# Attention and SwiGLU on one core: all transposes on TensorE instead of partly by DMA, and readouts split in two

## The chip, the cores and the metric

The kernel runs on one core of one Trainium2 chip. The metric is the device time of one execution in microseconds (us); a kernel's time is the median of its runs.

## The reference

Attention over 4 batches, 8 heads, 768 positions and a head dimension of 64, with two kinds of heads, and then a feed-forward block on the result. Everything is float32 in the reference; the kernel computes in float16 with float32 sums.

```python
scores = (q @ k^T) / sqrt(64)                       # q, k, v: (4, 8, 768, 64)
causal = row >= col
stream = causal & ((col < 4) | (row - col < 64))    # 4 sink keys, a window of 64
mask   = causal for heads 0, 2, 6; stream for the other five heads
a      = softmax(where(mask, scores, -1e9))
x      = (a @ v) as (3072 tokens, 512)
out    = (silu(x @ w_gate) * (x @ w_val)) @ w_out   # w_gate, w_val: 512 x 1536; w_out: 1536 x 512
```

## The kernel before

The 3072 tokens are 24 tiles `t` of 128 rows; two tiles make a pair `n` (12 pairs, in the order of `QP`), four tiles a group `g` (6 groups).

**Per pair.** `load` (L341) brings q, k and v of 256 rows into buffers of the ring `raw` (11 buffers, L169). `cast` (L429) writes q and k as float16 into a buffer `hq`. Then q and k have to be turned, so that the head dimension lies on the partitions. For pairs below `XPE = 5` (L336) that is done by TensorE: `transposes` (L469) issues 8 transposes of 128x128 for q and 8 for k into one PSUM bank each, and `evac` (L475) copies each bank out in two halves (ScalarE or VectorE). For pairs 5 to 11 it is done by DMA: `dmat` (L462) issues a transposing DMA on SyncE's queue, two for q and two for k of a pair. In the pairs whose turning is by DMA, q and k are loaded with 512 bytes in a run, one DMA each; pairs 1 to 4 are loaded with 2 KB in a run, two DMAs each, and cast into another order of columns (`XOLD <= n < XPE`).

**Per tile.** `scores` (L551) multiplies on TensorE into two PSUM banks (`sc`), `exps` (L569) takes the exponential on ScalarE into `e`, `mask` (L581) multiplies with 0 and 1 on VectorE or GpSimd, `values` (L591) multiplies with v, and `norm` (L600) divides by the sums and writes `xb`. Then `xb` is turned into `xt`, with the model dimension on the partitions: for tiles below `XBAR = 8` (L423) by `xtranspose` (L609) with 4 transposes on TensorE and one copy out of PSUM (`xevac`, L624), for tiles 8 to 23 by one transposing DMA (L615).

**Per group.** For each of 12 blocks `j` of the hidden dimension: `gate` (L755) with the gate weights, `tanh` (L763), `stt1` (L767), `gate` with the value weights, `stt2` (L773), which writes `h_sb`. The output product of groups 0 to 4 is done with seven block products instead of eight (`seventh`, L830, matmuls at L839), with sums of blocks of h made by `hsum` (L818, L826). The seven products are added up into `out_sb` by `gathered` (L850): `r1` is a plain copy; `c11`, `r6`, `r67`, `c21`, `r56`, `c22` and `c12` are VectorE additions of a PSUM bank and a cell of `out_sb` (L855). Group 5 has a plain product (`outproj`, L788). `store_half` and `store` write the result.

**The order of the work.** Nothing is scheduled while the kernel runs. Every piece above is a task of a plan; the string `ORDER` gives the order in which the tasks are issued, `WAYS` the engine of each, `SLOTS` its buffers. An engine works through its own instructions in that order, each waiting on semaphores. Tasks in `ORDER` that are no tasks of the plan are matmuls that only keep TensorE running (`warm`, L315). The 8 PSUM banks are shared by scores, values, gates, products and transposes.

Of the kernel before, what the change touches and what calls it, by code (L numbers as in the profile page):

```python
# [16 lines left out]
    "0306071W091U1V1X000A08xy1c0D0C01050B1d1e040gy01f1gzJ1i1h2021282922232B1j1r1s021p1q1w0F2C2D2E2F1b"  # L17
    "2A2L2M2N2O2X2f2g0m1Y1a1Z1t1u1v1k0h252h1l1m2W2c242G2H2I2d2e2l2m2i2j0G271n1o1y1z3C262P2Q2R0z2t3031"
    "2J0y8e8o2n2K102U2o2p3I3J2V8t8j8m8u8v8k8l8n1x2k8f8g8p8q2x382y8h8i118r8s8w8x138y8z9893909495999A33"
    "340n9D9E0E2Z3K3D3L3M3N149B9C9F969G9H972a9192322b2Y2q2r2s2u3R3S3W3X0k1C9c9d9e9h9i9j3U3V3O2z353P36"  # L20
    "39370q1D9f9g9k9l3T3b3i3n3o3f3g0H3H3E3F2v2w0i169I9J9K9N9O9P0o179L9Q9R9M0l1F3Q3Y3Z3c3j3a0I3u40410j"
    "193k3h9m9n9o3l3m3A3B9S9T9U9r9s9t3d3e9X0J3v4344453G3p3q3r0r1G9u9p9v429Y9Z3s3t0x1H2S4647494A4H0p1A"
    "9V9WB74N4O4Q4R0K3z9q9zA10N4c3x4BB4B5B6B8Ak4K4L4V4b4C4D3yAT484M0w0sAQARASAU9a9b9y0t1E0W6K2TAlAmAV"
    "AWAX151M1O1N1PAYAZBEAfAgAhB9BABB4a0u181Q1R1SBCBDAp0v1BBFBGA0AaAbAnAoAc3wBHBIAdAe0L0M0PB20T12A41I"
    "1J1K0S4d4P0O4Z4h4g4Y4e4f5D5L5K0RAzB0B1AqArB31L0YALAM0ZAN4E4F4G4J4I6J1TAuAvAOAPAw9wA2A69xA3A7A55C"
    "5I5JAA4l4m4i4j4kACA8A9ABAD4n4v51524y53AiAj5f5lAEBMAGAFAK4S4z504T4W4UAxAy5g5nAsAtBL4q4r4o4p54BO0c"
    "AHAIAJ4s554t4u4x4wBJBKBQ56575T5U6MBNBP5W5c5XBb5j0X58595A5B707S7T6xBVBW6wBRBS5i5VBXBYBc6z5YBZBaBd"
    "5p5qBT5s605t5u4XBsBtBuCeCbCcCdCfCMCNCOCCBvBwCDCE0V6I5v0Q5F5G5H6v5k5o5M5N5O0UBiBjBk5rCPCQBlBm5E5Z"
    "5a5b5d5wCHCICJCWCXCY5m63696A666768Bh5h73CKCLC7C8C9710eCRCS5P5Q5R6465CACBCTBUC2C36y7Q6P74BnBo5x5y"
    "5z610a72CZCaBp5S625e6H6NBqBrC46B6C6F6D6GCFCGCiBeBfBgBxByBz7O7UC0C1C5C681CUCVCjCl6E6U6V6W6X6Y6R6S"  # L30
    "6T6eDmDjDkDlDnDoDpDqDrDs0b7P7X7WDtDuDv6Z6aCgChCn6b6c6d6fDUDVDWDXDY7576776g7C7D7E7F7G7L0dDwDxCkCm"
    "DSDFDGDHDPDQDRDT7b7c7d6QDADBDCDyDzE0DDDE7H80D5D6D7CsCt6O6n6o6h6i6j6kE1E27V7I7J7M7K7ND8D96l6m7879"
    "7A7BCoCpCrCuCv897Y7Z6p6q8786DKDLDMDZDaDb6L6r6s6t6uDcDdDeDfDgCwCx7e7f7R7j7m7n7o7p7q7rDNDOCyCzD0D4"
    "EhEiEjErEsEcEd88EkElEtCqD1D2D3EuEvEeDhDi7a7g7h7k7iFLFMFNFOFP7x8D8E8A8I8B8C8F8JFJFGFHFIFKFBFCFDDI"
    "DJE5E77s7t8GFEFFEp7u7v7y7w8HEXEYEZ0f838485EmEnEoEqEfEg8NEw8Y8ZE6E88T8U8VEzExEyF0EBE3E9E4EAECEDF6"
    "828K8L8M8OF1F2F3F9EFEG8Q8R8S8W8XEVEHEIEJF7F8FA7l8P7z8a8b8cEaEbESETEUEWEEEOELEM8dGiGMGTGUEKGCENER"
    "G7GVGWGjGkGJGKEPGREQFTFVGXGLGOGPGEGFGNGQG9F4GAGSGGGYGbGZF5GaGcGBGDFSGHFpFqFrFQFRG4G5GdGeFzFUFeFW"
    "FXGIG6G0G8FcFdGfFfFuFvFYFaFbGgGhG1G2G3FsFtFxGlGmFZFwFyFlFiFjFmFnFgFhFkFoGnGoGpGsGtGuGvGwGqGrGxGy"
    "GzH0H2H3H4H5H7H1H6H8H9"
)  # L40
WAYS = (
    "000010000000000000000000000000000000000000000000000000000000221202202202212200200111000111110010"
    "222200001100000000000000220022122022001011000000000000001100212002000011001001000001000001001000"
# [76 lines left out]
def kernel(  # L120
# [45 lines left out]
    PAIRS = [(2, 6), (0, 4), (1, 5), (3, 7)]  # L166
    assert all(y == x + 4 for x, y in PAIRS)

    RINGS = {"raw": 11, "hq": 5, "e": 6, "xb": 3, "xt": 2, "sig": 2, "sil": 3,  # L169
             "ps": 8, "gv": 8, "o": 8, "big": 8}  # L170
    P = Plan(RINGS)

# [160 lines left out]

    XPE = 5  # L336
    XOLD = 1

    landed = {}
# [83 lines left out]
    XBAR = 8  # L423
# [596 lines left out]
```

## Time and profile before

| | |
|---|---|
| median of 3 runs | 246.04 us (245.84 to 246.38) |
| the profiled execution's own time | 246.15 us |
| its span, first to last instruction | 244.4 us |
| granted TensorE clock | 1.000 |
| TensorE busy | 234.5 us, 96% |
| VectorE busy | 186.7 us, 76% |
| ScalarE busy | 148.5 us, 61% |
| GpSimd busy | 129.0 us, 53% |
| DMA moved | 40.73 MB, 167 GB/s over the span |

In the profile PE is TensorE's matmul side, PEld its weight loads, DVE VectorE, ACT ScalarE, POOL GpSimd and SP SyncE, which here only issues DMAs. Matmuls overlap in a pipeline, so the busy time of PE is no measure of how full it is: the mean duration of a 512-column matmul is given as 379 ns, while one starts every 216 ns in a dense stretch. The chain of waits is followed back from the last instruction: each step to what released it, or to the instruction before it on its engine. "Issue" in it is time in which the profile shows nothing waited for.

### The profile page before, as it was taken

Reading aid. Unit: us, or ns where it says so; the run is one execution under the profiler, and the core shown is the slowest. Engines: PE = TensorE matmul, PEld = TensorE weight load, DVE = VectorE, ACT = ScalarE, POOL = GpSimd, SP = SyncE. Lnnn points to the kernel's source line nnn. Section 1 sums busy time; section 2 is a strip of 40 time slices with the busy share of each in tenths; the row PEclk is TensorE's granted clock in tenths of the full one; section 3 lists DMA queues with packets and bytes.
Section 4 is the critical chain, followed back from the end, with each engine's and each line's share of the span. In section 5 each row is a group of like instructions: output and inputs, shape, how many; then the busy total and the mean of one; then the engine's idle time right before and its main releaser. Section 6 shows DMA issues by size and latency. Waiting matters only on the chain.

```text
span 244.4 us, 5604 instructions
## 1 busy us (share of the span) xinstructions
PE 234.5 (96%) x2189; PEld 143.6 (59%) x2189; DVE 186.7 (76%) x324; ACT 148.5 (61%) x235; POOL 129.0 (53%) x140
## 2 busy tenths in 40 slices
PE   7989999998999999799999999999999999999995
PEld 3667855553457678445555457656456764475743
DVE  0577887889999999887987977669769777776800
ACT  3899899887878669487637776563682302330011
POOL 7479999956497552375765446910094110375000
PEclk9999999999999999999999999999999999999999
DMA  6999999999766989999464451519100213100053
GB/s 187 355 348 353 323 352 366 313 362 305 206 131 78 287 165 289 191 268 192 89 130 130 97 120 38 90 36 234 38 4 0 46 21 115 59 0 1 7 203 136
DMA packets 66794, 40.73 MB, mean 167 GB/s; under 512 B 25168, under 2 KB 60240, under 8 KB 66768
## 3 DMA queue, kind: packets, MB, share of 16 engines
q1 hardware_dynamic: 65392, 37.76, 61.5%
q10 hardware_dynamic: 1376, 2.62, 2.9%
q8 instruction: 17, 0.28, 0.5%
q14 instruction: 9, 0.07, 0.1%
HBM read 28.31 MB, written 6.29 MB: 142 GB/s over the span
## 4 chain that ended last, share of the span: by engine, by line
PE 54%; DVE 19%; issue 8%; DMA 6%; POOL 5%; SPq 5%; ACT 2%; DVEq 0%; POOLq 0%
PE banks L759 34%; PE banks L839 10%; PE banks L793 4%; DMA raw<-in_moe_w_val_dram 4%; DVE h_sb L775 4%; PE banks L567 3%; DVE h_sb L826 3%; SPq L349 3%; DVE sil L769 3%; PE banks L597 2%; POOL hs_sb L826 2%; DVE out_sb L855 2%; DVE xb L605 2%; DMA xt<-xb 2%; DVE e L587 2%
## 5 line engine op out<-in xcount | busy, mean ns | idle before, releaser
L759 PE MATMUL banks<-xt,wg_sb 128*128 128x512 f16 (+1 forms) x304 | 70.3, 368 | 1.9 <-DMA xt<-xb 1.4
L759 PE MATMUL banks<-xt,wv_sb 128*128 128x512 f16 (+1 forms) x304 | 70.4, 368 | 0.8 <-DVE sil L769 0.7
L579 ACT ACTIVATE e<-banks 128x1024 f16<-128x1024 f32 (+2 forms) x68 | 58.7, 910 | 20.0 <-PE banks L567 11.7
L765 ACT ACTIVATE sig<-banks 128x512 f32<-128x512 f32 (+1 forms) x76 | 43.0, 577 | 43.5 <-PE banks L759 37.5
L769 DVE SCALAR_TENSOR_TENSOR sil<-sig,banks 128x512 f32<-128x512 f32 (+1 forms) x76 | 49.0, 656 | 14.8 <-ACT sig L765 12.6
L775 DVE SCALAR_TENSOR_TENSOR h_sb<-sil,banks 128x512 f16<-128x512 f32 (+1 forms) x76 | 48.7, 656 | 6.7 <-PE banks L759 4.4
L587 POOL TENSOR_TENSOR e<-e,m 128x640 f16<-128x640 f16 (+1 forms) x22 | 37.8, 1727 | 27.2 <-ACT e L579 24.3
L759 PEld LDWEIGHTS <-wg_sb 128*128 128x128 f16 x304 | 28.5, 98 | 30.7 <-issue 3.1
L759 PEld LDWEIGHTS <-wv_sb 128*128 128x128 f16 x304 | 28.2, 98 | 29.5 <-issue 1.2
L839 PEld LDWEIGHTS <-h_sb 128*128 128x128 f16 x360 | 34.8, 98 | 7.9 <-issue 0.7
L826 POOL TENSOR_TENSOR hs_sb<-h_sb 128x768 f16<-128x768 f16 x7 | 11.5, 1640 | 40.9 <-DVE h_sb L775 29.4
L855 DVE TENSOR_TENSOR out_sb<-banks,out_sb 128x512 f32<-128x512 f32 x35 | 23.6, 685 | 4.7 <-PE banks L839 4.4
L826 POOL TENSOR_TENSOR h_sb<-h_sb 128x768 f16<-128x768 f16 x11 | 18.0, 1639 | 8.2 <-PE banks L839 4.4
L839 PE MATMUL banks<-wo_sb,h_sb 128*128 128x256 f16 x180 | 21.9, 273 | 0.0
L839 PE MATMUL banks<-wt_sb,h_sb 128*128 128x256 f16 x180 | 21.5, 273 | 0.4 <-DVE out_sb L855 0.4
L567 PE MATMUL banks<-qT,kT 64*128 64x128 f16 x472 | 20.6, 218 | 1.1 <-DVE xb L605 1.0
L567 PEld LDWEIGHTS <-kT 64*128 64x128 f16 x472 | 14.6, 94 | 11.0 <-issue 10.2
L597 PEld LDWEIGHTS <-e 128*128 128x128 f16 x472 | 17.1, 97 | 4.3 <-ACT vt L206 0.9
L597 PE MATMUL banks<-vt,e 128*128 128x65 f16 x472 | 18.2, 193 | 1.0 <-POOL vt L208 0.7
L605 DVE TENSOR_TENSOR xb<-banks,rc 128x512 f16<-128x512 f32 x24 | 16.6, 691 | 0.8
L208 POOL CAST vt<-raw 64x512 f16<-64x512 f32 x22 | 14.4, 654 | 4.8 <-DMA raw<-in_v_dram 2.3
L206 ACT COPY out_sb<-banks 128x512 f32<-128x512 f32 (+1 forms) x7 | 4.0, 570 | 19.1 <-PE banks L793 16.0
(60 smaller groups left out, 216.3 us busy)
## 6 DMA issues: line engine op xcount, KB each, us to landing
raw<-in_v_dram SPq DMA_DIRECT2D x12, 512.0 KB, 7.0
raw<-in_q_dram SPq DMA_DIRECT2D x8, 512.0 KB, 4.8
raw<-in_k_dram SPq DMA_DIRECT2D x8, 512.0 KB, 5.1
raw<-in_moe_w_gate_dram SPq DMA_DIRECT2D x6, 512.0 KB, 8.9
raw<-in_moe_w_val_dram SPq DMA_DIRECT2D x6, 512.0 KB, 8.4
raw<-in_moe_w_out_dram SPq DMA_DIRECT2D x6, 512.0 KB, 7.9
out_dram<-out_sb SPq DMA_DIRECT2D x6, 512.0 KB, 4.7
raw<-in_q_dram SPq DMA_DIRECT2D x8, 256.0 KB, 6.4
```

The lines of the kernel that those rows point to most:

```text
L567: nc.tensor.matmul(sc[:, c:c + n, :], weights, moving, start=first, stop=last)
L579: nc.scalar.activation(out=to, in_=src, func=AF.Exp, scale=scale)
L587: ENG[task().way].tensor_tensor(out=ev, in0=ev, in1=mm, op=ALU.mult)
L597: nc.tensor.matmul(avs[t][:, odd, n * 66:n * 66 + 65], ee, vv, start=(m == 0), stop=(m == len(bl) - 1))
L605: nc.vector.tensor_tensor(out=xb.rearrange("p n o d -> p o n d"), in0=av[:, :, :, 0:64], in1=rc.to_broadcast([128, 2, 4, 64]), op=ALU.mult)
L759: nc.tensor.matmul(ps, wsb[:, kk, j * 128:(j + 1) * 128], xt[:, kk, c[0]:c[1]], start=(kk == 0), stop=(kk == 3))
L765: nc.scalar.activation(out=sg[g, j, c], in_=gs[g, j, c], func=AF.Tanh, scale=0.5)
L769: nc.vector.scalar_tensor_tensor(out=sl[g, j, c], in0=sg.pop((g, j, c)), scalar=1.0, op0=ALU.add, in1=gs.pop((g, j, c)), op1=ALU.mult)
L775: nc.vector.scalar_tensor_tensor(out=hs[g, j][:, c[0]:c[1]], in0=sl.pop((g, j, c)), scalar=0.5, op0=ALU.mult, in1=vs.pop((g, j, c)), op1=A ...
L826: ENG[T_hs[g, x][part].way].tensor_tensor(out=to, in0=a, in1=b, op=op)
L839: nc.tensor.matmul(rooms[g, p][:, x], left[:, j, 128 * x:128 * x + 128], right[:, j], start=(j == 0), stop=(j == NK - 1))
L855: nc.vector.tensor_tensor(out=cell(*to), in0=rooms[g, p], in1=cell(*other), op=ALU.add)
```

## The change

- `XPE` becomes 12 and `XBAR` goes: q and k of all pairs and x of all tiles are turned by TensorE and copied out of PSUM. `dmat` and the transposing DMA of `xtranspose` go. With `XPE = 12`, q and k of pairs 5 to 11 are loaded in two DMAs with 2 KB runs, and the exponentials of their tiles write their columns in plain order.
- The additions `c11`, `c21` and `c12` of groups 0 to 4 become two tasks each: `fetched` copies the PSUM bank into a float32 buffer of a new ring `tmp` (two buffers) by ScalarE or VectorE, and `summed` adds that buffer and the cell of `out_sb` by GpSimd or VectorE. The PSUM bank is free after the copy.
- The ring `raw` has 10 buffers instead of 11.
- `ORDER`, `WAYS` and `SLOTS` are new as a whole.

What the new `WAYS` assign (number of tasks; before -> after):

| tasks | ScalarE | VectorE | GpSimd | SyncE |
|---|---|---|---|---|
| transposing DMAs of q and k | | | | 28 -> 0 |
| transposing DMAs of x | | | | 16 -> 0 |
| copies of turned k out of PSUM | 4 -> 15 | 6 -> 9 | | |
| copies of turned q out of PSUM | 8 -> 16 | 2 -> 8 | | |
| copies of turned x out of PSUM | 2 -> 8 | 6 -> 16 | | |
| `c11`, `c21`, `c12` as one addition | | 15 -> 0 | | |
| their copies (`fetched`) | 0 -> 6 | 0 -> 9 | | |
| their additions (`summed`) | | 0 -> 8 | 0 -> 7 | |

On TensorE, the tasks of 8 transposes go from 10 to 24, those of 4 transposes from 8 to 24, the `warm` matmuls inside the order from 11 to 14. Everything else on TensorE is the same in number and size. In the new order the first gate products again come after the scores and values of tiles 0 to 3, and the first load of value weights is again the eleventh load.

```diff
-    RINGS = {"raw": 11, "hq": 5, "e": 6, "xb": 3, "xt": 2, "sig": 2, "sil": 3,
+    RINGS = {"raw": 10, "hq": 5, "e": 6, "xb": 3, "xt": 2, "sig": 2, "sil": 3, "tmp": 2,
...
-    XPE = 5
+    XPE = 12
...
-    XBAR = 8
-
...
-    def dmat(n, kd, m):
-        nc.sync.dma_start_transpose(
-            out=turned(n, kd)[:, m].rearrange("c k r (j n) -> c (k r j) n", j=2),
-            in_=hqs[n, kd][m * 64:(m + 1) * 64].rearrange("p k a x -> p (k a x)"))
...
-        if t // 2 >= XPE:
-            to = to.rearrange("p c (n j) -> p c n j", j=2)
-            src = src.rearrange("p c (j n) -> p c n j", j=2)
         nc.scalar.activation(out=to, in_=src, func=AF.Exp, scale=scale)
...
-        if t >= XBAR:
-            nc.sync.dma_start_transpose(
-                out=xts[g][:, :, n * 128:(n + 1) * 128],
-                in_=xb.rearrange("p a b d -> p (a b d)"))
-            return
         tr = buf("gv", [128, 4, 128], FH, "xtr")
...
-            if n >= XPE:
-                T_ev[n, kd] = [P.lands(P.add(
-                    f"d{kd}{n}.{m}", ["SP"], (lambda n=n, kd=kd, m=m: dmat(n, kd, m)),
-                    deps=cs[kd] + old)) for m in range(2)]
-                P.uses(cs[kd][0], "hq", *T_ev[n, kd])
-                continue
...
+    APART, SINCE = ('c11', 'c21', 'c12'), 0
+
+    def fetched(g, name):
+        temps[g, name] = buf("tmp", [128, 2, HM], FP, "tmp")
+        copy(T_fe[g, name], temps[g, name], rooms[g, CELLS[name][0]])
+
+    def summed(g, name):
+        p, to, other = CELLS[name]
+        ENG[T_ga[g, name].way].tensor_tensor(out=cell(*to), in0=temps.pop((g, name)),
+                                             in1=cell(*other), op=ALU.add)
...
+            if name in APART and g >= SINCE:
+                T_fe[g, name] = P.add(f"fe{g}.{name}", ["ACT", "DVE"],
+                                      (lambda: fetched(g, name)), deps=deps[:1], takes=["tmp"])
+                T_ga[g, name] = P.add(f"oe{g}.{name}", ["POOL", "DVE"],
+                                      (lambda: summed(g, name)), deps=[T_fe[g, name]] + deps[1:])
+                P.uses(T_fe[g, name], "tmp", T_ga[g, name])
+                return T_ga[g, name]
...
-        P.uses(p2, "o", c11)
+        P.uses(p2, "o", T_fe.get((g, "c11"), c11))
...
-        P.uses(p4, "o", c21)
+        P.uses(p4, "o", T_fe.get((g, "c21"), c21))
...
-        P.uses(p3, "o", c12)
+        P.uses(p3, "o", T_fe.get((g, "c12"), c12))
```

## The prediction

> **What bounds the kernel now.** I read the page first, then stretches of the span, the chain of waits in order of time, and the groups.
>
> The page's first part:
>
> ```profile
> PE 234.5 (96%) x2189; PEld 143.6 (59%) x2189; DVE 186.7 (76%) x324; ACT 148.5 (61%) x235; POOL 129.0 (53%) x140
> ```
>
> Two stretches (columns: stretch, its length, then busy us and instruction count of PE, PEld, DVE, ACT, POOL, then clock, DMA share, GB/s):
>
> ```profile
> 60.00:100.00 40.00, 39.16 (x406) 27.35 (x404) 38.92 (x66) 29.84 (x44) 21.32 (x19) 1.00 0.90 188
> ...
> 200.00:241.40 41.40, 41.38 (x247) 23.40 (x244) 24.76 (x38) 9.29 (x16) 11.40 (x7) 1.00 0.19 71
> ```
>
> TensorE looks full, but its busy time is modelled. The chain shows what one matmul really takes back to back (start, length, what):
>
> ```profile
> 28.34 0.45 PE banks L473 x8
> ...
> 45.64 0.22 PE banks L621 x4
> ...
> 47.17 0.85 PE banks L597 x28
> ...
> 136.75 0.85 PE banks L567 x24
> ...
> 200.24 13.81 PE banks L759 x64
> ...
> 227.06 3.93 PE banks L839 x36
> 230.99 10.40 PE banks L793 x60
> 241.47 0.29 DVE out_sb L208
> ```
>
> So a 512-column matmul takes 13.81/64 = 0.216 us, a 256-column one 3.93/36 = 0.109, a q or k transpose 0.45/8 = 0.056, an x transpose 0.055, a score 0.85/24 = 0.035, a value matmul 0.85/28 = 0.030. With the counts of the groups: gates 544 x 0.216 = 117.4 and 64 of 256 columns x 0.109 = 7.0; products 420 x 0.109 = 45.9; the last product 10.4; scores 472 x 0.035 = 16.7; values 472 x 0.030 = 14.3; 80 + 32 transposes 4.5 + 1.8; masks put in by matmul (24) 2.3; warming 21 x 0.216 = 4.5. Sum 224.8 us of real work in 244.4.
>
> Where are the other 19.6? The first gates that run on without a break start at 22.65 on the chain, behind the first loads. The groups of the stretch up to there hold 16.0 us of this work (56 q and k transposes, 75 scores, 48 value matmuls, 16 x transposes, 8 gates, the 24 masks and all 21 warming ones). The opening thus has 6.6 us of waits. From 22.65 to TensorE's end at 241.39 lie 218.7 us with 208.8 of work: **9.9 us of waits**. The last 3.0 us are the end's copy and store. TensorE bounds the kernel after the opening, at 95% of its real rate.
>
> **The change part by part.** The sum is made against the profiled execution, 246.15 us (span 244.4 and 1.75 around it), 0.11 above the median.
>
> *Transposes.* q and k: 14 tasks of 8 by 0.0563 = 6.3 us. x: 16 tasks of 4 by 0.055 = 3.5 us. Together **+9.8 us on the engine that sets the end**; the opening can't take any of it, as the pairs concerned are loaded later.
>
> *The DMAs that go.* 44 transposing DMAs leave SyncE's queue. The rows of them and of those who wait:
>
> ```profile
> L615 SPq DMA_TRANSPOSE xt<-xb x16: 1188/1195/2348, 80.0 to 196.9; - x16
> L463 SPq DMA_TRANSPOSE kT<-hq x14: 1201/1286/2478, 68.3 to 164.0; - x14
> L463 SPq DMA_TRANSPOSE qT<-hq x14: 1193/1225/2070, 71.1 to 155.7; - x14
> ```
>
> The list of waits (us in total, times, longest) has one line of TensorE with them:
>
> ```profile
> PE banks L759 <- DMA xt<-xb: 1.4, 1, 1.4
> ```
>
> They held the queue for some 44 x 1.2 = 53 us (durations are minimum/median/maximum ns), but TensorE waited for one of them once, for 1.4 us. That wait goes: **-1.4**. A norm-to-gate path by TensorE, 0.22 and a copy of 0.42 to 0.59, is shorter than the 2.7 us of a landing, so nothing takes its place. Loads queued behind these DMAs go out earlier; who would gain is GpSimd (2.3 us of waits for v, 2.4 for q and k), which is idle for half the span, so I count nothing. In the last stretch shown TensorE has no wait left for any of this to remove.
>
> Here the Trainium skill takes the change's side. "VectorE: DVE Perf Modes", The three transpose paths, gives 390 ns for a 128x128 transpose on TensorE and 1309 ns by DMA, and its rules prefer TensorE where PSUM will do. As an estimate by that page, 176 transposes alone would be 69 us; the rows show 0.056 us each when they follow one another, and it is the row that a full engine pays. The page compares latencies, which the planned order hides in either case.
>
> *Copies out of PSUM.* By the table of ways: k 11 more on ScalarE and 3 on VectorE, q 8 and 6, x 6 and 10. ScalarE: 11 x 0.588 + 8 x 0.590 + 6 x 0.586 = 14.7 us. VectorE: 3 x 0.598 + 6 x 0.683 + 10 x 0.419 = 10.1 us.
>
> *Split readouts.* 15 additions of 0.685 leave VectorE, -10.3. But nine of the 15 copies are VectorE's own, by the 0.684 of its copy of 128x512 f32 from PSUM 6.2 us, and eight of the additions are. An f32 addition of two SBUF tiles isn't in the trace. The nearest rows are the block sums, also with two SBUF inputs:
>
> ```profile
> L826 DVE TENSOR_TENSOR h_sb<-h_sb x9: 548/559/1746, 54.3 to 205.3; 128x768 f16<-128x768 f16 x9
> ...
> L855 DVE TENSOR_TENSOR out_sb<-banks,out_sb x35: 670/684/693, 80.4 to 231.8; 128x512 f32<-128x512 f32 x35
> ```
>
> The addition from PSUM never varies; the one from two SBUF tiles takes 0.55 us or up to 1.75. So 0.55 to 1.75 each; I take 0.83, the mean over VectorE's 19 block sums (15.8 us): 6.6. VectorE's balance is -10.3 + 6.2 + 6.6 = **+2.5: the split doesn't relieve it**. ScalarE gets 6 x 0.585 = 3.5. GpSimd gets 7 additions, between the 1.16 us of its 128x512 f16 subtraction and the 1.64 of 128x768: 8.1 to 11.5; it is idle for 115 us. Whether a bank that frees sooner helps TensorE: it waited 0.6 us for a readout in all, so between nothing and -0.6; I take 0.
>
> A page speaks against this part. "SBUF — State Buffer", SBUF: two separate sides, says that a VectorE instruction with two SBUF inputs and a GpSimd one that reads SBUF exclude each other for a whole instruction. The long block sums agree (1.746 against 0.548). As an estimate by that rule every one of the eight additions could meet a GpSimd one, 8 x 1.2 = 9.6 us on VectorE; my term has a mean wait of 0.27 each, 2.2.
>
> *The rest of the plan.* Other tasks changed engines (casts, masks, block sums). Valued by the same rows, VectorE ends 11.2 us up, ScalarE 17, GpSimd 6. VectorE would then be busy 198 us of some 254, 78% against 76%, ScalarE 65%. In the stretch from 60 to 100 us VectorE is nearly full already (38.92 of 40). That decides the upper end.
>
> *Smaller edits.* Plain columns of the exponentials: 1024 columns take 1.025 us before and 1.024 after 85 us, so 0. Loads in two pieces: 14 more issues of 0.6 us in a queue that loses 53, 0. Ten landing buffers: a load starts one buffer later; cover is the DMA share of 0.32 after 140 us, and if it were gone, one landing, at most the 8.9 us median of the gate weights. Three more warming matmuls, 0.65 us: in the opening's 6.6 us of waits, 0.
>
> Sum: 246.15 + 9.8 - 1.4 = 254.5. The 8.5 us of waits left are waits in an in-order queue, and q and k transposes need only a cast, so they can stand where TensorE would wait; I take half a microsecond for that: **254.0**.
>
> **The rivals.**
>
> *VectorE or ScalarE becomes the bound* (slower still). The stretches at 38.92 of 40 speak for it, the averages of 78% and 65% against. If half of VectorE's 11.2 us lies where TensorE waits for it, 254.0 + 5.6 = 259.6; between 257 and 263.
>
> *The waits vanish* (not slower). One mechanism: transposes and copies fill just the places in which TensorE waits now. With no wait at all after the opening the time is 22.65 + 208.8 + 9.8 + 3.0 + 1.75 = 246.0, no change. It decides only when the 9.9 us fall to below 0.5, and for a gain the opening has to shorten too, which lies on the loads; the new order has the same eleven loads up to the first value weights, with 14 issues of 0.6 us ahead of them instead of 15. Price 244.5 to 247. The last stretch, without waits, shows that it is possible for 41 us; 60 to 200 us speaks against it.
>
> *The split does what its words say* and takes all 15 additions from VectorE. The ways speak against it (nine copies, eight additions); it would give 254.0 less 0.6. It lies inside the forecast's case.
>
> **How the numbers follow.** The forecast, TensorE pays for its transposes and keeps between 3 and 11 us of waits, 248 to 257: 0.70. VectorE or ScalarE as the bound, 257 to 263: 0.20. No waits, 244.5 to 247.5: 0.10, of which 0.06 gains over 0.2%, 0.03 is within it, and 0.01 is slower. 0.2%, half a microsecond, is about what a measurement of this kernel can tell from no change. So faster 0.06, same 0.03, slower 0.91. The range for 8 in 10 runs from 248.0 to 260.0: it leaves out the tenth below and the top half of the second case.
>
> **What would show it.** Right: the transposes at L473 and L621 counted 192 and 96, spaced by 0.056 in the chain; TensorE's real work at 235; its waits after the first gates 6 to 10 us; no DMA among what TensorE waits for; the end near 252 in the span. VectorE's additions with two SBUF inputs spread from 0.55 to over 1.5 us. Wrong: if TensorE's matmuls run faster than the spacings above, if the waits fall under 2 us, or if the first steady gates start earlier than 21 us. If the span passes 256, TensorE's list of waits will name VectorE or ScalarE in the stretch 60 to 140.

## The result, and the profile after

The changed kernel takes 262.83 us (median of 4 runs, 261.99 to 264.59) against 246.06 us for the kernel before: a ratio of **1.069 [1.063, 1.075]**. Slower, as predicted, but by 16.8 us instead of 8: 2.8 us above the top of the range, and inside the bounds given for the rival in which VectorE or ScalarE becomes the bound (257 to 263).

The profiled execution took 262.28 us, with a span of 260.5. The busy line of its page:

```profile
PE 247.7 (95%) x2368; PEld 154.1 (59%) x2368; DVE 203.5 (78%) x348; ACT 164.2 (63%) x264; POOL 138.1 (53%) x146
```

By shares nothing has happened: 96% became 95%, 76% became 78%. That is the first thing to see: the loss doesn't show in any engine's share. VectorE is up 16.8 us, ScalarE 15.7, GpSimd 9.1; predicted were 11.2, 17 and 6. The surpluses on VectorE and on GpSimd are a first hint: the prediction's rows already had a block sum of VectorE's last 1.75 us instead of 0.55, and such a longer instruction counts as busy.

Where the 8.3 us beyond the predicted sum went can be worked out as the prediction did it. The first gates on the chain start at 22.06 us (22.65 before) and TensorE ends at 257.46, so 235.4 us lie between. The 0.6 us are no gain: 8 of the q and k transposes, 8 scores, 4 x transposes and 8 gate matmuls of 256 columns that were done by then before are still to come, 1.8 us. The work behind 22.06 is 208.8 + 9.8 + 1.8 = 220.4 us. That leaves **15.0 us of waits**, where the prediction left 8.0 (9.9 less 1.4 less 0.5). The opening is 1.2 us worse (1.8 - 0.6): half of that is the three more warming matmuls (0.65 us), which the prediction put at nothing. 15.0 - 8.0 + 1.2 = 8.2.

The price of a transpose and the counts were right; three pieces of the chain of waits (start, length, what):

```profile
22.06 1.03 PE banks L734 x8
...
92.57 0.45 PE banks L468 x8
...
247.06 10.40 PE banks L768 x60
```

Eight transposes take 0.45 us still, and the last product 10.40 us, to the hundredth what it took before. Now the stretches after the opening (stretch, length, busy us and count of PE, PEld, DVE, ACT, POOL, clock, DMA share, GB/s):

```profile
60.00:100.00 40.00, 37.33 (x366) 24.29 (x365) 36.54 (x61) 31.43 (x51) 26.12 (x22) 0.96 0.46 148
100.00:140.00 40.00, 39.97 (x397) 25.20 (x396) 33.97 (x60) 29.59 (x49) 21.36 (x20) 1.00 0.32 104
140.00:200.00 60.00, 58.52 (x584) 35.01 (x583) 49.96 (x82) 39.01 (x62) 23.37 (x24) 1.00 0.11 36
200.00:257.00 57.00, 55.68 (x396) 34.54 (x394) 39.26 (x60) 15.95 (x28) 19.14 (x12) 1.00 0.16 60
```

From 60 to 100 us TensorE is busy for 37.33 of 40 us (39.16 before), and after 200 us, where it was at 41.38 of 41.40, it is at 55.68 of 57. TensorE's entries in the list of waits (us in total, times, longest), without the shorter ones and the opening's wait for `ident`:

```profile
PE banks L734 <- DVE sil L744: 2.9, 3, 2.2
...
PE banks L589 <- DVE e L579: 1.3, 1, 1.3
PE banks L734 <- DVE h_sb L750: 1.2, 2, 1.1
PE banks L562 <- DVE xb L597: 1.2, 2, 0.9
PE banks L734 <- DVE xt L210: 0.5, 1, 0.5
```

In the list of before, VectorE's entries are these:

```profile
PE banks L759 <- DVE sil L769: 1.1, 3, 0.4
PE banks L567 <- DVE xb L605: 1.0, 2, 0.5
PE banks L839 <- DVE out_sb L855: 0.6, 2, 0.4
```

No DMA is left, as predicted, and **VectorE is named for every listed wait after the first gates**: 6.3 us (the wait for `xt` and 0.3 of those for `xb` are the opening's), where it was 2.7 before. Of the 15.0 us the list holds these 6.3; 1.8 more are a short fall of the clock in this execution (told at the end), and 6.9 lie in gaps too short to be listed and in what the spacings above don't cover, against 5.8 before. What grew is thus first what VectorE is named for, +3.6, and then the clock, +1.8.

The longest wait, 2.2 us at 74 us, shows its cause in the timeline (start, length, engine, line, what, count, idle time before and its releaser):

```profile
71.71 2.52 DVE L414 TENSOR_TENSOR wt_sb<-wo_sb,wt_sb 128x512 f16<-128x512 f16 x2 [0.45 <-POOL wt_sb L414]
...
72.74 2.50 POOL L414 TENSOR_TENSOR wt_sb<-wo_sb 128x512 f16<-128x512 f16 x2
...
74.15 1.50 DVE L801 TENSOR_TENSOR h_sb<-h_sb 128x768 f16<-128x768 f16 x1
...
75.58 1.27 DVE L744 SCALAR_TENSOR_TENSOR sil<-sig,banks 128x512 f32<-128x512 f32 x2
76.30 1.02 PE L734 MATMUL banks<-xt,wv_sb 128*128 128x512 f16 x4 [2.20 <-DVE sil L744]
```

VectorE adds two pairs of output-weight blocks in 2.52 us, although one such addition takes 0.42 alone; GpSimd does the same kind of work at the same time. Then a block sum of 0.55 takes 1.50, and only then comes the `sil` that frees the bank for TensorE's next value gate. VectorE is busy all the while, and held up for most of it. The same operations over the whole kernel, with VectorE's masks of before (L587) behind them (durations are minimum/median/maximum ns):

```profile
L801 DVE TENSOR_TENSOR h_sb<-h_sb x9: 548/558/2389, 74.2 to 238.4; 128x768 f16<-128x768 f16 x9
...
L579 DVE TENSOR_TENSOR e<-e,m x19: 481/692/2120, 35.1 to 205.7; 128x640 f16<-128x640 f16 x10, 128x1024 f16<-128x1024 f16 x9
...
L414 DVE TENSOR_TENSOR wt_sb<-wo_sb,wt_sb x4: 418/825/1258, 71.7 to 80.0; 128x512 f16<-128x512 f16 x4
...
L840 POOL TENSOR_TENSOR out_sb<-tmp,out_sb x8: 1265/1269/1279, 97.5 to 249.0; 128x512 f32<-128x512 f32 x8
L840 DVE TENSOR_TENSOR out_sb<-tmp,out_sb x7: 680/684/1856, 88.2 to 218.1; 128x512 f32<-128x512 f32 x7
```

```profile
L587 DVE TENSOR_TENSOR e<-e,m x16: 482/678/1360, 44.5 to 191.9; 128x1024 f16<-128x1024 f16 x10, 128x640 f16<-128x640 f16 x6
```

The minima are those of before; the maxima have grown (block sums 1746 to 2389, masks 1360 to 2120). The lines of the additions (L840) also correct a count: eight of the 15 additions are GpSimd's and seven VectorE's, not the other way round as in the table of ways above and in the prediction.

One figure used below sums this up: for every VectorE TENSOR_TENSOR with two inputs in SBUF, its time beyond the shortest of its shape. **Before: 6.8 us over 39 instructions. After: 13.0 us over 52.** This is called the hold-up. The 6.2 us more are near the surplus of VectorE's busy time over the predicted one (16.8 - 11.2 = 5.6). Masks have 3.9 of them, weight sums 1.3, the seven new additions 1.2; the block sums are 0.3 lower. That GpSimd is the holder can be read from the trace: all 16 of these instructions that ran more than 0.1 us over their shortest (11 of 11 before) lie beside GpSimd's work for at least as long as they are too long, while 26 of the 36 others have no GpSimd work beside them. GpSimd's casts are among the holders, not only its sums and masks.

A second place, late in the kernel, where the prediction expected no waits:

```profile
203.92 1.86 DVE L840 TENSOR_TENSOR out_sb<-tmp,out_sb 128x512 f32<-128x512 f32 x1
...
205.31 4.01 POOL L801 TENSOR_TENSOR h_sb<-h_sb 128x768 f16<-128x768 f16 x2
...
205.70 2.12 DVE L579 TENSOR_TENSOR e<-e,m 128x1024 f16<-128x1024 f16 x1
...
207.87 0.81 PE L589 MATMUL banks<-vt,e 128*128 128x65 f16 x21 [1.32 <-DVE e L579]
```

One of the new additions (0.68 alone, here 1.86) and a mask (0.69, here 2.12) stand beside GpSimd's block sums, and the values wait 1.32 us for the mask.

Last, **where along the kernel the time is lost**: if both traces are laid side by side at equal progress of TensorE's common work (transposes and warming left out), the changed kernel is 2.9 us late at 70 us of the old time, 7.3 at 80, 8.2 at 92, 10.5 at 124, 13.0 at 175 and 16.1 at 207. More than a quarter of the loss, 4.4 us, arises in the ten microseconds after 70; 2.2 of it are the wait above, and 1.8 are the fall of the clock in this execution.

### The profile page after: what moved, and what is told of

Its sections match the earlier page's. It is cut to its first block, busy times and chain, and to the rows that moved or that the text cites. A ratio compares the mean times of both kernels' runs of the same rounds, so it can differ in the third digit from the quotient of the medians.

```text
span 260.5 us, 5990 instructions
## 1 busy us (share of the span) xinstructions
PE 247.7 (95%) x2368; PEld 154.1 (59%) x2368; DVE 203.5 (78%) x348; ACT 164.2 (63%) x264; POOL 138.1 (53%) x146
## 4 chain that ended last, share of the span: by engine, by line
PE 80%; DVE 12%; POOL 3%; issue 3%; ACT 1%; POOLq 0%; ACTq 0%
PE banks L734 39%; PE banks L814 18%; PE banks L562 6%; PE banks L589 5%; PE banks L768 4%; PE banks L468 3%; PE banks L323 3%; DVE e L579 2%; PE banks L608 2%; POOL wt_sb L414 1%; DVE xb L597 1%; DVE h_sb L750 1%; DVE sil L744 1%; DVE vt L214 1%; DVE wt_sb L414 1%
## 5 line engine op out<-in xcount | busy, mean ns | idle before, releaser
L734 PE MATMUL banks<-xt,wv_sb 128*128 128x512 f16 (+1 forms) x304 | 71.6, 368 | 4.0 <-DVE sil L744 2.9
L734 PE MATMUL banks<-xt,wg_sb 128*128 128x512 f16 (+1 forms) x304 | 71.5, 371 | 0.7 <-DVE xt L210 0.5
L579 POOL TENSOR_TENSOR e<-e,m 128x1024 f16<-128x1024 f16 (+1 forms) x19 | 35.2, 1859 | 34.2 <-ACT e L571 34.0
L814 PE MATMUL banks<-wo_sb,h_sb 128*128 128x256 f16 x180 | 22.8, 279 | 0.0
L801 POOL TENSOR_TENSOR h_sb<-h_sb 128x768 f16<-128x768 f16 x11 | 18.8, 1721 | 5.5 <-DVE h_sb L801 2.9
L210 POOL CAST vt<-raw 64x512 f16<-64x512 f32 x26 | 17.2, 664 | 3.2 <-DMA raw<-in_v_dram 1.9
L830 DVE TENSOR_TENSOR out_sb<-banks,out_sb 128x512 f32<-128x512 f32 x20 | 13.5, 689 | 5.8 <-POOL out_sb L840 3.0
L210 POOL CAST hq<-raw 128x1024 f16<-128x1024 f32 (+1 forms) x14 | 12.5, 913 | 9.6 <-PE banks L468 8.8
L597 DVE TENSOR_TENSOR xb<-banks,rc 128x512 f16<-128x512 f32 x24 | 16.6, 691 | 1.1 <-DVE rc L596 0.4
L801 POOL TENSOR_TENSOR hs_sb<-h_sb 128x768 f16<-128x768 f16 x4 | 6.6, 1641 | 20.5 <-DVE h_sb L750 20.4
```

The costliest lines, as they stand in the source:

```text
L210: ENG[task.way].tensor_copy(out=dst, in_=src)
L579: ENG[task().way].tensor_tensor(out=ev, in0=ev, in1=mm, op=ALU.mult)
L597: nc.vector.tensor_tensor(out=xb.rearrange("p n o d -> p o n d"), in0=av[:, :, :, 0:64], in1=rc.to_broadcast([128, 2, 4, 64]), op=ALU.mult)
L734: nc.tensor.matmul(ps, wsb[:, kk, j * 128:(j + 1) * 128], xt[:, kk, c[0]:c[1]], start=(kk == 0), stop=(kk == 3))
L801: ENG[T_hs[g, x][part].way].tensor_tensor(out=to, in0=a, in1=b, op=op)
L814: nc.tensor.matmul(rooms[g, p][:, x], left[:, j, 128 * x:128 * x + 128], right[:, j], start=(j == 0), stop=(j == NK - 1))
```

## The experiments

Four readings were set against each other, together or in part: that TensorE's own added work sets the time; that the copies out of PSUM fill VectorE and ScalarE; that VectorE and GpSimd hold each other up; and that the new order itself is worse. "The old plan" is `ORDER`, `WAYS` and `SLOTS` of before, with the tasks that an edit adds put in next to those that they replace or feed. All ratios are to the kernel before, measured beside it. Differences to the changed kernel are taken from its median, whose interval is 1.5 us to either side. The code is shortened. Each expectation stands as it was recorded before its run; in them theory A is TensorE's work with VectorE's hold-ups, B the copies, B' VectorE's queue as a whole, C the new order.

### One part of the change alone, in the old plan

**old_T**: transposes by TensorE and nothing else of the change.

```diff
-    XPE = 5 ... XBAR = 8
+    XPE = 12 ... XBAR = 24       # no transposing DMA
     ORDER: d{k}{n}.{m} -> tr{k}{n} ev{k}{n}.{m};  xdma{t} -> xtr{t} xe{t}
```

> The old plan with the new transposes alone: the 44 transposing DMAs of the kernel before are replaced, where they stood, by the 176 transposes on TensorE and their 44 copies out of PSUM, with the engines that the changed kernel gives these copies; readouts stay whole, 11 landing buffers, nothing else moves. Theory A (TensorE pays 9.8 us for the work; what lies above 254 in the changed kernel are VectorE's instructions with two SBUF inputs held up by GpSimd in the new plan): 246.1 + 9.8 - 1.4 = 254.5, between 252 and 257. Theory B (the 44 copies out of PSUM make VectorE and ScalarE the bound): 259 to 265, as in the changed kernel. Theory C (the new order is simply worse): 254.5, as A.

263.19 us, 1.068 [1.066, 1.071]: +17.0, as much as the whole change. The hold-up grows only to 9.4 us, with no new addition in it, so a great part of the loss needs neither the split nor the new order.

**old_S**: the split readouts alone, with the ten landing buffers.

```diff
+    c11, c21, c12 -> fetched + summed          # as in the change
-    RINGS raw: 11
+    RINGS raw: 10, tmp: 2
```

> The old plan with the split readouts alone: c11, c21 and c12 of groups 0 to 4 become a copy and an addition at the place of the old addition, on the engines that the changed kernel gives them (6 copies on ScalarE, 9 on VectorE; 7 additions on VectorE, 8 on GpSimd), and the landing buffers are 10. Transposes as before. Theory A: the new additions with two SBUF inputs collide with GpSimd's work, 1 to 4 us: 247 to 250. Theories B and C: within 0.7 us of 246.1, since VectorE's balance is 2.5 us and most of it beside TensorE's work.

256.65 us, 1.0418 [1.0392, 1.0444]: **+10.5**, the costliest surprise, since the prediction had priced the split at 2.5 us of VectorE that nobody waits for. Its list of waits, and then its timeline at 170 us:

```profile
POOL out_sb L865 <- DVE tmp L208: 18.2, 3, 10.0
...
PE banks L597 <- POOL e L587: 2.6, 1, 2.6
```

```profile
170.03 0.68 DVE L208 COPY tmp<-banks 128x512 f32<-128x512 f32 x1
...
170.79 1.26 POOL L865 TENSOR_TENSOR out_sb<-tmp,out_sb 128x512 f32<-128x512 f32 x1 [9.97 <-DVE tmp L208]
...
172.01 2.12 POOL L587 TENSOR_TENSOR e<-e,m 128x1024 f16<-128x1024 f16 x1
...
174.19 0.89 PE L597 MATMUL banks<-vt,e 128*128 128x65 f16 x19 [2.61 <-POOL e L587]
```

GpSimd sat at its addition for 9.97 us until VectorE's copy was there; a mask was queued behind the addition, and TensorE's values behind the mask. The addition costs 1.26 us; the hand-over costs TensorE 2.61. The rest of the 10.5 isn't taken apart; TensorE's list also has 3.8 us for `sil` (1.1 before) and 1.2 for a copy of ScalarE's into `tmp`.

**old_dummy**: the old plan with its DMAs kept, and TensorE doing the 176 transposes as well into banks that nobody reads.

```diff
+    dm = P.add(f"dum{kd}{n}", ["PE"], (lambda: transposes(n, kd)), deps=cs[kd], takes=["gv"])
+    dumx{t}: 4 transposes of xb                # t >= 8
```

> The old plan, its transposing DMAs and its copies as before, and beside them 176 transposes on TensorE whose results nobody reads, at the places (and nearly all in the banks) that the run with the new transposes alone gave them. It shows what TensorE's work costs without the copies. That run took 263.2, 17 us over the kernel before. Theory A (the work itself): 254 to 256, and the other 7 to 9 are what the copies, the banks held until they are done, and the waits of scores and gates for them add. Theory B (all comes from the copies; TensorE has room): 246 to 250. If the places are bad in themselves, by transposes that wait for their casts in TensorE's queue: 259 to 263.

257.70 us, 1.0466 [1.0444, 1.0488]: **+11.4 for 9.8 us of work**. TensorE pays in full for its transposes and 1.6 us more; its list has 1.4 us in which transposes wait for `sil`, for their places and banks. From here to old_T are another 5.5 us, for the copies out of PSUM and what goes with them: old_T has 2.1 us of waits for ScalarE's `qT` (0.2 here). It also loads q and k in other pieces, and no run parts the two.

### The new plan with parts taken away

**new_noT**: the new plan with the transposes done by DMA.

```diff
+    XPE = 5, XBAR = 8
+    ORDER: tr/ev/xtr/xe -> the transposing DMA, right after what it needs
```

> The changed kernel with its transposes of pairs 5 to 11 and tiles 8 to 23 by DMA again, each DMA issued right after what it needs in the new order; the split readouts and all other places stay. Theory A: 262.8 - 9.8 and a little for late landings: 252 to 255. Theory B: the copies go too, and with them the waits: 245 to 249. Theory C: 252 to 255.

319.81 us, 1.296 [1.289, 1.303]. A miss: put there, the DMAs stand in front of loads in SyncE's queue, TensorE's waits of up to 13.4 us follow, and even the granted clock falls to 0.92. It says nothing on the transposes.

**light**: one transpose of eight (q, k) or of four (x) is done in the pairs and tiles that are new on TensorE, so most of `kT`, `qT` and `xt` isn't transposed; the copies keep their size.

```diff
-        for j in range(8):
+        for j in range(8 if n < 5 else 1):
-        for p in range(4):
+        for p in range(4 if t < 8 else 1):
```

> The changed kernel with 1 of 8 transposes for each q and k of pairs 5 to 11 and 1 of 4 for each x of tiles 8 to 23; the copies out of PSUM keep their number and size and read the one turned block again and again, so this part of the result isn't computed. It takes 112 x 7/8 x 0.056 + 64 x 3/4 x 0.055 = 8.2 us of work from TensorE and nothing from any other engine. Theory A (TensorE bounds): 262.8 - 8.2 = 254.6, between 253 and 256.5. Theory B (the copies bound): 259 to 262.

260.60 us, 1.059 [1.0555, 1.0625]: **8.2 us of TensorE's work taken away, 2.2 us gained.** Compare old_dummy: in the old plan the same work costs all it takes. In the changed kernel TensorE is not what sets the time alone. The hold-up rose from 13.0 to 15.5 us.

**light_copies**: the copies of those transposes write two columns, so most of `kT`, `qT` and `xt` isn't written; the transposes stay whole.

```diff
-        copy(T_ev[n, kd][m], dst, trs[n, kd])
+        copy(T_ev[n, kd][m], dst[:, 0:2], trs[n, kd][:, 0, 0:2])     # n >= 5; x alike, t >= 8
```

> The changed kernel with all its transposes on TensorE, but the copies out of PSUM of pairs 5 to 11 (save k of pair 5) and of tiles 8 to 23 copy two columns each, so the rest of what they would bring isn't brought and the products use what lay there. It takes some 7 us of work from VectorE and 9 from ScalarE, none from TensorE. The run with fewer transposes gave 260.6, 2.2 below the changed kernel for 8.2 us less on TensorE, and eight additions moved to VectorE cost 4.4 for 5.5 us. Theory B', from these two (in the new plan VectorE's queue, not TensorE, sets the pace): 254 to 257. Theory A (TensorE bounds): 261 to 263.

262.64 us, 1.0665 [1.0634, 1.0696]: some 7 us less of work on VectorE and 9 on ScalarE are worth 0.2, which is no measurable difference. That the copies fill the two engines fell as a theory. The hold-up rose to 15.6.

**light_both**: both cuts (k of pair 5 keeps its eight transposes).

> Both cuts at once: 1 of 8 and 1 of 4 transposes, and copies of two columns. What is left over the kernel before is the split readouts and the new order itself. If either resource alone would hold the time, and both together give it back: 246 to 250. If the new order costs by itself: 251 to 256.

260.80 us, 1.0594 [1.0561, 1.0626]: 2.0 us. The two cuts together do no more than the first. Where they went, the lines of VectorE's two-input operations tell:

```profile
L810 DVE TENSOR_TENSOR h_sb<-h_sb x9: 549/589/2378, 73.8 to 236.8; 128x768 f16<-128x768 f16 x9
...
L585 DVE TENSOR_TENSOR e<-e,m x19: 484/693/2441, 34.8 to 204.5; 128x640 f16<-128x640 f16 x10, 128x1024 f16<-128x1024 f16 x9
...
L417 DVE TENSOR_TENSOR wt_sb<-wo_sb,wt_sb x4: 418/1241/1906, 71.4 to 79.6; 128x512 f16<-128x512 f16 x4
```

The same instructions last longer: the median weight sum 1241 ns (825), the longest mask 2441 (2120). The hold-up is 18.4 us, 5.4 more than in the changed kernel: VectorE lost some 7 us of work and is held for 5.4 us more.

**new_noS**: 11 of the 15 split readouts made whole again, one product in another bank.

```diff
-    APART, SINCE = ('c11', 'c21', 'c12'), 0
+    APART = [(0, 'c21'), (1, 'c21'), (2, 'c12'), (2, 'c21')]
```

> The changed kernel with 11 of the 15 split readouts made whole again, one VectorE addition from PSUM each (the other four, c21 of groups 0 and 1 and c12 and c21 of group 2, stay split, since their banks are taken again before the sum can be made); one product gets another bank. Everything else in its place. Theory A, with what the split alone showed in the old plan (256.7, 10.5 us up, with GpSimd and ScalarE waiting for VectorE's copies and work queued behind): it costs here too, though less as this plan was made for it: 257 to 261. If the new plan hides it: 262 to 264, or more where banks free later.

267.64 us, 1.0867 [1.0845, 1.089]: 4.8 us worse than the change. In the old plan the split costs 10.5 us, in the plan made for it undoing most of it costs 4.8. So the price of the split is a property of the order around it.

### Moving work between the engines

**adds_dve**: GpSimd's eight additions to VectorE.

```diff
     oe0.c12 oe1.c11 oe1.c21 oe2.c11 oe2.c12 oe4.c11 oe4.c21 oe4.c12: POOL -> DVE
```

> The changed kernel with the eight additions of GpSimd on VectorE, nothing else. VectorE gets 8 x 0.7 = 5.5 us of work; GpSimd loses 8 x 1.27 = 10 us, its waits for copies in the middle of its queue, and with them eight occasions on which it holds up VectorE's block sums, masks and additions. If hand-overs to GpSimd and collisions are what the split costs: 259 to 262. If VectorE's load is: 264 to 267.

267.25 us, 1.0855 [1.0811, 1.0899]: +4.4 for 5.5 us more on VectorE, although GpSimd lost 10 us and its hand-overs. Added work on VectorE costs four fifths of its length here, though removed copies brought nothing. The hold-up is 14.7 us: the additions are held on VectorE as well.

**copies_act**: 18 of VectorE's copies of turned q, k and x to ScalarE.

> The changed kernel with the 18 copies of turned q, k and x that VectorE does for pairs 5 to 11 and tiles 8 to 23 on ScalarE instead, in the same places. VectorE loses 11 x 0.42 + 4 x 0.68 + 3 x 0.60 = 9.1 us, ScalarE gains 18 x 0.59 = 10.6 of its idle 96. Theory B': 256 to 260. If copies in ScalarE's queue come late behind exponentials and tanh, and gates and scores wait for them: 262 to 267.

266.36 us, 1.0813 [1.0795, 1.0831]: +3.5, with the hold-up down to 10.5. ScalarE has the time but not at the right moment: TensorE's list has new waits for it, 1.4 us for `kT` at 106 us, 0.7 for `qT` at 98, 0.6 for `vt` and 0.3 for `kT`. From 92.7 to 99.6 us ScalarE works through casts and copies one after another, and the piece of `kT` waited for at 106 us stands behind two casts and three copies of `xt`.

**after_ways**: three of GpSimd's block sums and masks and two of its weight sums, those beside which VectorE was held, to VectorE.

```diff
     ws1.0 ws3.0 mask22.0 hs3.2.1 hs3.4.1: POOL -> DVE
```

> The changed kernel with five tasks moved from GpSimd to VectorE and nothing else: two weight sums (ws1.0, ws3.0), one mask (mask22.0), two block sums (hs3.2.1, hs3.4.1). They are those that ran on GpSimd while a VectorE instruction with two SBUF inputs lasted 1.3 to 2.4 us, just ahead of the three longest waits of TensorE (at 74, 191 and 206 us: 2.4, 1.2 and 1.5 us). VectorE gets some 2.6 us more work. Theory A: these waits shrink, -2 to -5 us: 258 to 261. Theory B: more work on a full engine, 262.8 to 265. Theory C: 262 to 264.

261.96 us, 1.0635 [1.0612, 1.0658]: 0.9 better, which the intervals don't tell from no change. The waits at 191 and 206 us shrink and `sil` falls from 2.9 to 1.4 us in TensorE's list, but a new entry stands at 78.6 us, `DVE wt_sb`, 3.0 us once. The wait moved along VectorE's queue.

### Taking GpSimd's work away

**light_pool**: GpSimd's masks, block sums (but for the first two of group 0) and additions work on an eighth of their columns or fewer, so most of their results are left out; their instructions and hand-overs stay. **before_pool** is the same cut in the kernel before.

```diff
+        if task().way == "POOL":
+            ev, mm = ev[:, :, 0:16], mm[:, :, 0:16]
...
+        if T_hs[g, x][part].way == "POOL" and (g, x) != (0, 1):
+            to, a, b = (z[:, :, 0:32] for z in (to, a, b))
...
+        few = slice(0, 32 if T_ga[g, name].way == "POOL" else HM)     # light_pool alone
```

> The changed kernel with GpSimd's masks, block sums (save the first group's first two) and additions on an eighth or less of their columns, so that part of each isn't computed; VectorE's stay whole, and so do all transposes, copies and casts. GpSimd loses some 67 us, and with them most of the time in which it holds up VectorE. If VectorE's hold-ups by GpSimd (13.0 us) and late GpSimd results hold the changed kernel's time: TensorE becomes the bound that the prediction took, 252 to 256, and the hold-ups fall under 3 us. If the new order holds it in another way (loads, PSUM banks, ScalarE): 259 to 262.

> The control: the same cut in the kernel before (its masks and block sums on GpSimd; it has no split additions). If GpSimd holds up only the new plan: 244 to 246. If both plans suffer from it alike: 237 to 242.

light_pool 255.83 us, 1.0393 [1.0367, 1.0418]; before_pool 244.00 us, 0.9908 [0.9873, 0.9943]. **The cut is worth 7.0 us in the changed kernel and 2.3 in the one before**, and neither ScalarE's nor VectorE's tasks were touched. A block sum, one stretch, and TensorE's waits of light_pool:

```profile
L805 DVE TENSOR_TENSOR h_sb<-h_sb x9: 548/553/1501, 71.3 to 231.9; 128x768 f16<-128x768 f16 x9
```

```profile
140.00:200.00 60.00, 60.00 (x608) 36.91 (x606) 48.47 (x85) 40.59 (x64) 10.39 (x25) 1.00 0.14 45
```

```profile
PE banks L818 <- DVE wt_sb L414: 0.9, 1, 0.9
PE banks L736 <- DVE sil L746: 0.9, 1, 0.9
PE banks L562 <- DVE xb L599: 0.7, 2, 0.4
```

The hold-up is 5.3 us instead of 13.0 (1.2 in before_pool), the wait of 2.2 us is down to 0.9, and TensorE is busy for all of the 60 us after 140. GpSimd's weight sums and casts keep their size, and they are what VectorE is still held by. The hold-up fell by 7.7 us and the time by 7.0. The cut also shortens what waits for GpSimd's results themselves, so this bounds the hold-up's price from above.

Nor is the hold-up a price by itself: copies_act has 10.5 us of it and is 3.5 us slower than the changed kernel with 13.0, and before_ways (below) has 8.9 and is no slower than the kernel before with 6.8. What counts is whether TensorE waits for the instruction that is held.

**bare**: light_both and light_pool together.

> The changed kernel with all three cuts: one transpose in eight or four, copies of two columns, GpSimd's masks, sums and additions narrow. If transposes, copies and GpSimd together make the difference: at or below what the same GpSimd cut leaves of the kernel before, 238 to 247. If the new order costs by itself: over 250.

250.98 us, 1.0192 [1.0162, 1.0223]. Once most of GpSimd's work is out of the way, the cuts of light_both are worth 4.85 us instead of 2.0. That is what the two theories that fell singly had right: the transposes and copies do cost, but while VectorE is held up, that hides them.

Still, bare is 7.0 us behind before_pool. About 2 of it are transposes left on TensorE beyond those of before (21 of q and k, 16 of x: 37 x 0.056). **The other 5 us aren't taken apart**: bare still has the new order and ways, the split readouts, the loads in other pieces, short copies out of PSUM, and a hold-up of 5.2 us against 1.2. Beside the kernel before (not before_pool), at equal progress bare is 1.7 us late at 70 us, 4.4 at 80 and 4.7 at the end. Its trace tells what TensorE waits for between 70 and 80 us, 0.9 us for a `sil` at 73 us and 0.9 for a weight sum at 78:

```profile
PE banks L827 <- DVE wt_sb L417: 0.9, 1, 0.9
```

```profile
L417 DVE TENSOR_TENSOR wt_sb<-wo_sb,wt_sb x4: 428/1065/1259, 69.5 to 77.5; 128x512 f16<-128x512 f16 x4
```

VectorE's weight sums are held there by GpSimd's weight sums and casts, which this cut leaves whole. light_pool has the same two waits.

### The place at 70 to 80 us

In the new order output-weight sums of group 0's product stand at this place, and six of the twelve are VectorE's (four before).

**ws_late**: product p4 of group 0 after p6 and p7, in another bank, and two weight sums of VectorE's later.

```diff
     ORDER: out0.p4 (bank 1) after out0.p7;  ws2.0 ws4.0 after hs0.2.1;  fe0.c21 after p4
```

> The changed kernel with the order around 74 us mended: the product p4 of group 0 comes after p6 and p7 instead of second, into another bank, and the weight sums ws2.0 and ws4.0 on VectorE come after the block sum hs0.2.1 in the order, so that VectorE's sil products of group 1 no longer stand behind them. No engine's work changes. If the order of these sums makes the lag of 4.4 us at 80 us: 258.5 to 261.5, and TensorE's wait of 2.4 us at 74 goes. If the lag comes from the sum of VectorE's and GpSimd's work in that stretch: 262 to 264, with the wait a little later.

265.35 us, 1.0771 [1.0732, 1.081]: 2.5 worse. In its list of waits:

```profile
PE banks L734 <- DVE sil L744: 2.9, 3, 2.2
PE banks L734 <- DVE h_sb L750: 2.1, 3, 1.1
```

The wait of 2.2 us stayed and others came, 0.8 us for `h_sb` at 83 us and 0.9 for `xb` at 87. So the theory that the place of these two sums makes the wait fell.

**ws_late_ways**: the same, with `mask22.0`, `hs3.2.1` and `hs3.4.1` moved from GpSimd to VectorE.

> The same, and mask22.0, hs3.2.1 and hs3.4.1 on VectorE instead of GpSimd. In the run with five moves the waits at 191 and 206 us shrank while another of 3.2 us came up at 79, and 0.9 us were won in all. If the later places are worth 1.5 to 2.5 us by themselves: that much below ws_late. If TensorE's list of waits only shifts: within 0.7 us of it.

262.81 us, 1.0684 [1.0648, 1.072]: 2.5 below ws_late, and the waits of 1.06 us for `h_sb` at 191 and 1.32 for `e` at 206 us are gone, as in after_ways. This supports a second time that those two waits come from GpSimd's instructions standing beside VectorE's. But the kernel is no faster than the changed one, with a hold-up of 9.8 us instead of 13.0.

### A version that beats both

**before_ways**: the kernel before with six small tasks (five casts of v and one copy of sink values) moved from VectorE to GpSimd and a cast of output weights to ScalarE.

```diff
     cx4.0.1 cx5.1.1 cx7.1.0 cx9.0.0 cx10.1.1 sv3.4: DVE -> POOL;  wc o3: -> ACT
```

> The kernel before with seven tasks taken from VectorE and nothing else: five casts of v (cx4.0.1, cx5.1.1, cx7.1.0, cx9.0.0, cx10.1.1) and one copy of sink values (sv3.4) to GpSimd, one weight cast (wc o3) to ScalarE. VectorE loses 5 x 0.68 + 0.98 + 1.21 = 5.6 us, most of it between 55 and 100 us, where it is busy 38.9 of 40. If VectorE sets the pace there: 243.5 to 245.7. If TensorE does: 245.9 to 246.6. If GpSimd, being slower to start behind its masks, delivers late: 246.6 to 248.

245.53 us (10 runs), **0.9973 [0.9958, 0.9989]**: 0.7 us faster than the kernel before, by an interval that just leaves out 1, and the fastest whole kernel here. **before_ways2** moves four more to ScalarE.

> The kernel before with the seven moves of the run that gave 245.53 and four more from VectorE to ScalarE: three casts of v (cx7.1.1, cx9.0.1, cx11.1.0) and a copy of sink values (sv1.4), 3 us of VectorE's time. If VectorE still paces the stretches at 91, 108, 118 and 180 us: 244.5 to 245.5. If TensorE does there: 245.3 to 245.8. If ScalarE's exponentials come late behind them: 246 to 247.

246.05 us, 0.9995 [0.998, 1.001]: no gain is seen, though the two intervals overlap a little.

## Why the prediction was right and where it failed

**Right.** The direction, and the mechanism for part of it. TensorE pays for its transposes: 11.4 us in old_dummy for 9.8 of work, and with most of GpSimd's masks, sums and additions out of both kernels, light_pool and before_pool stand 11.8 us apart. The price of 0.056 us, the counts, the work of 235 us, no DMA left in TensorE's waits, the remaining need of VectorE despite the split, and the sign to look for if the span passed 256 (VectorE in TensorE's list between 60 and 140 us) all came true. The mean of an addition with two SBUF inputs on VectorE, taken as 0.83 us, came out at 0.85. Two of the signs for being right failed: 15.0 us of waits instead of 6 to 10, and the end at 260.5 us instead of near 252.

**The step that failed** is "The 8.5 us of waits left are waits in an in-order queue", with the half microsecond taken off them. They were carried over from the kernel before as if the change would leave them alone. They came out at 15.0 us instead of 8.0. VectorE is named for 6.3 of them, 2.7 before, since the change lengthened VectorE's queue in work and in hold-ups; 1.8 are the clock, and what made the unlisted rest stays open. Three things behind this step were mis-sized, and the warming matmuls in the opening (0.65 us at nothing; the opening is 1.2 us worse) make a small fourth:

- *The exclusion of VectorE and GpSimd, 2.2 us on VectorE, at nothing for the path.* The hold-up grew by 6.2 us. By light_pool less before_pool, at most 7.0 - 2.3 = **4.7 us** of the time hang on it; the intervals of these runs leave some 2 us to either side. The prediction had the right rows, the 1746 beside the 548, and the Trainium skill's "SBUF — State Buffer", SBUF: two separate sides, says that whichever of the two starts first keeps the shared ports for its whole instruction. The traces agree: 2389 ns at the longest against 548 at the shortest, beside a GpSimd instruction of 2.13 us. But it was applied to the additions alone, and there it was too much: the seven on VectorE were held for 1.2 us. The rest came at masks (3.9 us) and weight sums (1.3), less 0.3 at the block sums: GpSimd's whole list (9.1 us longer) meets all 52 of VectorE's two-input instructions, of which the new plan has 13 more. The 9.6 us worked out for the case that every addition is held are nearer to the whole growth than 2.2, but by luck: they are for the wrong instructions.
- *The copies out of PSUM, 14.7 and 10.1 us at nothing*, with average shares of 78% and 65% as cover. In the old plan they cost up to 5.5 us on top of the transposes (old_T less old_dummy, with the other loads in it). In the changed kernel cutting them alone gives 0.2, while the hold-up rises from 13.0 to 15.6. The share was no cover: part of the busy time is being held, and copies_act shows that idle time can stand at the wrong place.
- *The new order, priced by its totals.* bare leaves some 5 us that neither the transposes and copies nor the cut part of GpSimd's work explain. How much of them is the order itself isn't shown. Nothing in the prediction looked at what stands next to what in the new `ORDER`, although the stretch of 60 to 100 us had been named as the full one.

The whole slowdown can be laid out in one way of taking things off, in this order: 4.7 us for GpSimd's cut work beyond what the same cut brings before, then 4.85 for transposes and copies that are in the way, then 7.0 left (2 for transposes not cut, 5 not taken apart); 16.6 together. Another sequence of cuts gives other parts (transposes and copies first: 2.0), because each bottleneck covers the next.

**The rivals.** The time fell into the bounds of "VectorE or ScalarE becomes the bound", but its mechanism holds only in part: more VectorE work lengthens the kernel (adds_dve), and less VectorE and ScalarE work doesn't shorten it (light_copies). VectorE together with GpSimd is the bound in places, TensorE in others. That no waits would be left was wrong. The split by itself costs 10.5 us in the old plan, while in the new one undoing 11 of its 15 costs 4.8.

**What stays open.** Why bare is 5 us behind before_pool when the remaining transposes are taken off. Between 70 and 80 us it falls back by 2.7 us against the kernel before, and its trace names two waits for VectorE there, 1.8 us in all, beside weight sums and casts of GpSimd's. That points to the hold-up that is left, but no run takes these sums away. ws_late moved two of VectorE's weight sums and didn't remove the wait. Also open is how a planned order with only the transposes would do: old_T is an insertion into an old order, and its 17.0 us hold some loss from that.

## What to carry to other kernels

Price added work on the resource that it will queue for, not on an engine's share: here VectorE's two-input SBUF instructions and GpSimd's work were such a resource in part (16 of 52 were held), and time in which VectorE is held counts as busy. Before a hand-over to an idle engine is priced at the instruction's length, look at what stands behind it in that engine's queue, and who waits for that. And when a cut brings less than its size, look for the same instructions lasting longer before concluding that the work was hidden: in light_both some 7 us less work on VectorE stand beside 5.4 us of longer instructions, and in bare the same cut is worth 4.85 us instead of 2.0 once most of the holder's work is gone.

## What the runs showed of the hardware

- A VectorE block sum of two SBUF inputs lasted 2389 ns, 4.4 times its minimum, beside a GpSimd instruction of 2.13 us, and is shown as one busy instruction.
- GpSimd's addition of two 128x512 f32 tiles took 1.27 us, little more than its f16 subtraction (1.16), while VectorE's took 0.68.
- After TensorE's wait of 2.2 us at 74 us the granted clock fell for some microseconds (mean 0.96 from 60 to 100 us). Two more pieces of the chain show it: four gate matmuls in 1.87 us (0.86 elsewhere), twelve product matmuls in 2.05 (1.31).

```profile
77.50 1.87 PE banks L734 x4
79.36 2.05 PE banks L814 x12
```

The profiled runs of ws_late_ways and light_both have a wait of 2.20 us at the same place and a mean clock of 1.00 from 60 to 100 us, so the wait alone doesn't decide it. Two of the changed kernel's four runs had a mean clock of 0.993, and they were the shorter ones (262.28 and 261.99, against 263.38 and 264.59 at a clock of 1.000), so the dip isn't what made the difference to the kernel before.
